# One buffer for all V tiles, the last ones handed over in halves, and an earlier K load, in a decode attention kernel that streams K and V

## Chip, cores, metric

The kernel runs on one core of a Trainium2 chip. The metric is the device time of one execution in microseconds (us). The intervals quoted are 95% intervals.

## The reference

Attention for one new token: 32 query heads, 8 K/V heads, 65,536 keys, head size 128, bf16. Per K/V head `g` there are 4 query heads.

```python
B, Hq, Hkv, Sq, Sk, D = 1, 32, 8, 1, 65536, 128
scores = jnp.einsum("bhqd,bhkd->bhqk", q, k) * D ** -0.5     # k, v repeated 4 times over heads
p = softmax(scores, axis=-1)
out = jnp.einsum("bhqk,bhkd->bhqd", p, v)
```

K and V are 268.4 MB together and every byte is used once. So the question is always the same: is the queue of loads ever empty, and what happens after the last byte has landed?

## The kernel before

Each head has two K tiles and two V tiles of 8.39 MB, written here K(g,b) and V(g,b) or short K10. The buffer `io` has three places of one tile: place 0 for V, places 1 and 2 for K(g,0) and K(g,1). VectorE transposes a K tile in place in four pieces of 4.4 us. TensorE scores it (64 matmuls in a loop of 8 trips, with register addresses), then multiplies the V tile of the head before (64 matmuls in a static block, `wide`). Between heads come the maximum, the exponential on ScalarE and the transposed weights.

A load can be issued only when its place has been used. `s_sc` counts scored eighths of K, `s_vc` counts used V tiles. The loads, all issued in order by SyncE:

```python
    def load_k(g, b):
        SP.wait((s_sc, 16 * g - 8 + 8 * b if g else 0))
        load(k, g, b, 1 + b, (s_ka, s_kb)[b])

    def load_v(g, b):
        if g < G - 1:
            SP.wait((s_vc, 2 * g + b))
            load(v, g, b, 0, s_v[0])
            ...
        elif b == 0:                       # V(7,0): into the place of K(7,0)
            SP.wait((s_sc, 16 * g + 8))
            for i in range(2):
                load(v, g, b, 1, s_u[i], 128 * i, 128 * i + 128)
        else:                              # V(7,1): into the V place, in six cuts
            SP.wait((s_vc, 2 * g))
            ...
    load_k(0, 0); load_k(0, 1); load_v(0, 0)       # on one line each in the kernel
    load_k(1, 0); load_k(1, 1); load_v(0, 1)
    for g in range(2, G):
        for b in range(2):
            load_k(g, b)
            load_v(g - 1, b)
    load_v(G - 1, 0)
    load_v(G - 1, 1)
```

The TensorE loop, cut to its frame. `head_slot` is the argument that sets the slot of the loop's first instruction; with `head_slot={PE: 0}` the loop is called aligned below:

```python
    with nc.Fori(0, G + 1, 1, engines=OrderedEngineSet([PE]), head_slot={PE: 0}) as h:
        ...                                      # wait; add up the last head; zero PSUM by 5 matmuls
        with pe.Fori(0, 2) as j:
            with pe.If(h < G):
                with pe.Fori(0, 8) as n: ...     # scores: 8 matmuls a trip
            with pe.If(h * 2 + j > 1):
                take(s_et, 2)
                with pe.If(h * 2 + j == 2 * G):  # V(7,0), which lies in a K place
                    with pe.Fori(0, SL // UN) as n:
                        ...                      # register addresses
                        for c in range(4):
                            i = pe.matmul(out=vacc[0:16, :, :], ...)
                with pe.Else():
                    ...                          # 64 x wide(ch, tt)
```

## Time and profile before

| | before |
|---|---|
| time, median of 3 first runs (range) | 655.73 us (655.61 to 658.28) |
| span of the profiled run | 655.3 us |
| load queue's share of 16 DMA engines | 94.9% |
| TensorE, VectorE busy | 57%, 52% |
| holes in the loads | 100 to 112 us, and from 636 us to the end |

In the profiles PE is TensorE, DVE is VectorE, ACT is ScalarE; PEq and SPq are the sequencers of TensorE and SyncE, which issue instructions and loads. L339 is line 339 of the kernel.

The page of the profile, in lines: the span; the DMA engines' busy share in 40 slices of 16.4 us, in tenths, and the rate; two queues (packets, MB, share); then two groups of instructions (line, engine, operation, output and inputs, count, busy us, mean ns of one, idle time before them).

```profile
span 655.3 us, 7257 instructions
...
DMA  9999991999999999999999999999999999999970
GB/s 382 448 448 400 436 444 68 448 448 413 420 448 444 440 396 448 444 444 392 448 448 444 424 412 448 444 444 392 445 448 444 416 420 448 448 436 396 443 330 0
...
q1 hardware_dynamic: 5480, 268.44, 94.9%
...
q8 instruction: 1, 0.02, 0.0%
...
L339 PE MATMUL vacc<-io,et 128*16 128x512 bf16 x956 | 55.7, 387 | 5.3 <-PEq L325 5.3
...
L390 PE MATMUL vacc<-io,et 128*16 x64 | 16.7, 384 | 9.6 <-PEq L325 9.6
```

The loads are what fills the time. Two slices stand out: the seventh (68 GB/s) and the last (0). In between 27 tiles pass from 113 to 636 us, that is 433 GB/s, with no moment of 0.3 us or more in which no load is in flight. An estimate from that rate: at 433 GB/s, 268.4 MB take 620 us.

The table of windows shows both holes (columns: window; its length; busy time and count of TensorE, its weight loads, VectorE, ScalarE, GpSimd; granted TensorE clock, as a share of full speed; DMA share; GB/s):

```profile
100.00:112.00 12.00, 9.38 (x88) 3.92 (x88) 0.68 (x2) 0.00 (x0) 0.00 (x0) 1.00 0.00 0
112.00:116.00 4.00, 0.00 (x0) 0.00 (x0) 4.00 (x3) 0.00 (x0) 0.00 (x0) 1.00 1.31 524
...
632.00:636.00 4.00, 2.35 (x10) 0.85 (x10) 0.00 (x0) 0.00 (x0) 0.00 (x0) 1.00 0.97 387
636.00:655.00 19.00, 11.01 (x98) 4.42 (x96) 3.23 (x9) 0.00 (x0) 0.00 (x0) 0.91 0.01 5
```

A window counts each packet of a load whole, where it starts. In the stream a 64 KB packet takes 2.42 us (median) and most of the 16 DMA engines start theirs together, so windows of 2 to 4 us can show shares over 1 (524 GB/s) or low rates with no change in the flow. A hole is certain only where nothing is in flight.

And the timeline tells what ends each (start, duration, engine, line, instruction; in brackets the idle time before it):

```profile
82.32 17.42 DVE L227 STREAM_TRANSPOSE io<-io 128x4096 uint32<-128x4096 uint32 x4 [6.72 <-DMA io<-in_k_dram]
...
107.64 3.63 PE L339 MATMUL vacc<-io,et 128*16 128x512 bf16 x64 [0.27 <-PEq L325]
111.32 0.33 SPq L128 DMA_DIRECT2D io<-in_v_dram  x1
...
642.57 1.02 PE L390 MATMUL vacc<-io,et 128*16 x4 [0.70 <-PEq L325]
645.50 4.92 PE L339 MATMUL vacc<-io,et 128*16 128x512 bf16 x60 [1.91 <-PEq L325]
...
652.88 0.35 SPq L290 DMA_DIRECT2D out_dram<-o  x1
```

V(0,1) can be issued only at 111.32, when V(0,0) has been used; that waits for K(1,0), which was transposed from 82.32 on, when it landed. At the end, the register-addressed loop for V(7,0) needs 1.7 us for every four matmuls (27.3 us for 64, where the static block of V(6,1) took 3.63 us) and is still at work at 642.57. All but a trickle of the loads had landed by 636.2.

### The profile page before, as it was taken

How to read it: one execution, taken by the hardware profiler on the slowest of the kernel's cores; microseconds unless marked ns; L12 is line 12 of the kernel's file. 1: busy time of each engine (PE TensorE's matmuls, PEld its weight loads, DVE VectorE, ACT ScalarE, POOL GpSimd, SP SyncE). 2: the span in 40 equal slices, each digit the busy share in tenths (PEclk: the TensorE clock that was granted, in tenths of full speed). 3: DMA queues.
4: the chain of work that ended last, by engine and by line, in shares of the span. 5: the costliest groups of instructions: out<-in, count | busy, mean ns of one | idle time of the engine just before them, and what ended most of it. 6: DMA issues, size and time to landing. Idle time of an engine off the chain costs nothing. (4 is left out here: it accounts for less than half of the span.)

```text
span 655.3 us, 7257 instructions
## 1 busy us (share of the span) xinstructions
PE 376.2 (57%) x2167; PEld 147.6 (23%) x2167; DVE 342.4 (52%) x226; ACT 23.6 (4%) x65; POOL 7.9 (1%) x40
## 2 busy tenths in 40 slices
PE   1187466764818656284744838266580866628655
PEld 0032122221303222031311313122130322203212
DVE  1588192936439292564808466193733829156201
ACT  0000100010000100001000010001000010000100
POOL 1000000000000000000000000000000000000000
PEclk9999769795978879597895959879596886959898
DMA  9999991999999999999999999999999999999970
GB/s 382 448 448 400 436 444 68 448 448 413 420 448 444 440 396 448 444 444 392 448 448 444 424 412 448 444 444 392 445 448 444 416 420 448 448 436 396 443 330 0
DMA packets 5589, 268.50 MB, mean 410 GB/s; under 512 B 720, under 2 KB 720, under 8 KB 1104
## 3 DMA queue, kind: packets, MB, share of 16 engines
q1 hardware_dynamic: 5480, 268.44, 94.9%
q10 hardware_dynamic: 104, 0.02, 0.0%
q14 instruction: 4, 0.03, 0.0%
q8 instruction: 1, 0.02, 0.0%
HBM read 268.44 MB, written 0.01 MB: 410 GB/s over the span
## 5 line engine op out<-in xcount | busy, mean ns | idle before, releaser
L370 PE MATMUL sc<-io,wz 128*128 x1024 | 272.5, 418 | 217.0 <-PEq L325 174.6
L227 DVE STREAM_TRANSPOSE io<-io 128x4096 uint32<-128x4096 uint32 x64 | 279.5, 4415 | 109.4 <-DMA io<-in_k_dram 109.4
L370 PEld LDWEIGHTS sc<-io,wz 128*128 x1024 | 106.0, 104 | 386.8 <-issue 308.6
L263 DVE STREAM_TRANSPOSE et<-ex 128x512 bf16<-128x512 bf16 x32 | 21.5, 701 | 117.3 <-PE vacc L339 81.3
L339 PE MATMUL vacc<-io,et 128*16 128x512 bf16 x956 | 55.7, 387 | 5.3 <-PEq L325 5.3
L232 DVE TENSOR_REDUCE mx<-sc 128x1 f32<-128x512 f32 x32 | 20.8, 668 | 49.7 <-PE sc L370 49.7
L252 ACT ACTIVATE ex<-sc,nmb 128x512 bf16<-128x512 f32 x32 | 21.6, 685 | 589.8 <-DVE nmb L249 589.8
L339 PEld LDWEIGHTS vacc<-io,et 128*16 128x16 bf16 x956 | 24.6, 91 | 36.3 <-issue 14.1
L390 PE MATMUL vacc<-io,et 128*16 x64 | 16.7, 384 | 9.6 <-PEq L325 9.6
L356 PE MATMUL sc<-zero 128*128 128x512 bf16 x36 | 17.0, 628 | 0.0
L272 DVE TENSOR_SCALAR vs<-vacc,sely 128x128 f32<-128x128 f32 x8 | 2.8, 350 | 24.6 <-PE vacc L339 24.6
L352 PE MATMUL pb<-ls,sel 128*4 128x4 f32 x18 | 1.8, 169 | 19.1 <-PEq L325 19.1
L212 POOL COPY wz<-qT 32x16 bf16<-32x16 bf16 x32 | 6.1, 191 | 520.0 <-PE sc L370 516.7
L414 PE MATMUL pb<-one,nrow 1*128 1x1 f32 x16 | 2.8, 241 | 14.3 <-PEq L325 14.3
L390 PEld LDWEIGHTS vacc<-io,et 128*16 x64 | 5.5, 86 | 21.2 <-issue 17.9
L335 PE MATMUL pf<-vs,sel 128*4 128x128 f32 x20 | 4.2, 295 | 9.9 <-PEq L325 9.2
L275 DVE SCALAR_TENSOR_TENSOR vs<-vacc,sely,vs 128x128 f32<-128x128 f32 x24 | 8.4, 351 | 0.9
L252 ACT ACTIVATION_READ_ACCUMULATOR ex<-sc,nmb 128x1 f32 x32 | 6.5, 202 | 0.0
L352 PEld LDWEIGHTS pb<-ls,sel 128*4 128x4 f32 x18 | 1.2, 86 | 21.6 <-issue 21.4
L414 PEld LDWEIGHTS pb<-one,nrow 1*128 1x128 f32 x16 | 2.3, 182 | 15.6 <-issue 15.6
L356 PE MATMUL vacc<-zero 128*128 128x512 bf16 x9 | 5.7, 634 | 0.0
L356 PEld LDWEIGHTS sc<-zero 128*128 128x128 bf16 x36 | 3.9, 131 | 5.3 <-issue 5.0
(29 smaller groups left out, 23.9 us busy)
## 6 DMA issues: line engine op xcount, KB each, us to landing
io<-in_v_dram SPq DMA_DIRECT2D x3, 4096.0 KB, 38.0
io<-in_v_dram SPq DMA_DIRECT2D x1, 2048.0 KB, 23.6
io<-in_v_dram SPq DMA_DIRECT2D x1, 1024.0 KB, 25.7
io<-in_v_dram SPq DMA_DIRECT2D x1, 512.0 KB, 26.4
io<-in_v_dram SPq DMA_DIRECT2D x2, 256.0 KB, 26.7
io<-in_k_dram SPq DMA_DIRECT2D x16, 47.7
io<-in_v_dram SPq DMA_DIRECT2D x14, 28.9
out_dram<-o ACTq DMA_DIRECT2D x7, 1.0 KB
```

The lines of the kernel that those rows point to most:

```text
L212: gp.tensor_copy(out=wz[r, :, c0:c0 + H].rearrange("p (s w) h -> p s w h", s=2), in_=qTb[r, :, :, g, :],).then_inc(s_w, 1)
L227: dve.transpose(out=part.bitcast(u32), in_=part.bitcast(u32)).then_inc(s_kt, 2)
L232: return DV.mark(dve.tensor_reduce(out=mx[:, b:b + 1], in_=sc[:, 512 * b:512 * b + 512], axis=AX.X, op=ALU.max))
L252: a = act.activation(out=ex[:, b, :], in_=sc[:, 512 * b:512 * b + 512], func=ACT.Exp, bias=nmb[:, :], scale=SCALE, accum_out=ls[:, b:b + 1],)
L263: dve.transpose(out=et[:, i, :], in_=ex[:, 2 * b + i, :]).then_inc(s_et, 1)
L275: i = dve.scalar_tensor_tensor(out=vs[:, :], in0=vacc[:, y, :], scalar=sely[:, y:y + 1], in1=vs[:, :], op0=ALU.mult, op1=ALU.add,)
L335: return pe.matmul(out=fin, lhsT=sel[:, :], rhs=vs[:, :], skip_group_check=True, **kw)
L339: return pe.matmul(out=vacc[32 * c:32 * c + 16, :, :], lhsT=et[:, ch // 2, w0:w0 + 16], rhs=io[:, PS * ch + 4 * tt:PS * ch + 4 * tt + 4, : ...
L356: pe.matmul(out=bank, lhsT=zero[:, 0:P], rhs=zero[:, :], start=True, stop=False, skip_group_check=True,)
L370: i = pe.matmul(out=bass.AP(sc, r_o, [[2048, P], [1, 512]]), lhsT=bass.AP(wz, r_w + ((2 * s + e) * WB - 4 * u), [[4 * WB, P], [1, P]]), rh ...
L390: i = pe.matmul(out=vacc[0:16, :, :], lhsT=bass.AP(et, r_e + c * 32, [[1024, P], [1, 16]]), rhs=bass.AP(io, r_v + c * (4 * D), [[IO, P], [ ...
L414: pe.matmul(out=pb[:, 0:1], lhsT=nrow[:, :, :].rearrange("o x h -> o (x h)"), rhs=one[:, :], start=True, stop=True,).then_inc(s_pe, 1)
```

## The change

Its intent: no hole near 100 us, and no slow loop at the end. V(7,0) and V(7,1) go through the V place like all others. So that the V place does not become a bottleneck at the end, the last V tiles are handed over in halves (`s_vc` now counts half tiles), and K(7,1) comes in quarters. K(0,0) comes in halves and K(1,0) is loaded ahead of V(0,0). Zeroing PSUM moves from TensorE to ScalarE and VectorE, and the softmax of a head is put ahead of collecting the output of the head before. The loop is not aligned any more. The core of the diff:

```diff
+    k_cuts = {(0, 0): [0, 128, 256], (G - 1, 1): [0, 64, 128, 192, 256]}
...
     def load_v(g, b):
-        if g < G - 1:
-            SP.wait((s_vc, 2 * g + b))
+        done = 2 * (2 * g + b)
+        if (g, b) == (G - 1, 1):
+            SP.wait((s_vc, done - 1))
+            load(v, g, b, 0, s_v[0], CUTS[0], CUTS[1])
+            SP.wait((s_vc, done))
+            for lo, hi, s in list(zip(CUTS, CUTS[1:], s_v))[1:]:
+                load(v, g, b, 0, s, lo, hi)
+        elif (g, b) in ((G - 2, 1), (G - 1, 0)):
+            for i in range(2):
+                SP.wait((s_vc, done - 1 + i))
+                load(v, g, b, 0, s_v[i], 128 * i, 128 * i + 128)
...
     load_k(0, 0)
     load_k(0, 1)
-    load_v(0, 0)
-    load_k(1, 0)
-    load_k(1, 1)
-    load_v(0, 1)
-    for g in range(2, G):
+    for g in range(1, G):
         for b in range(2):
             load_k(g, b)
             load_v(g - 1, b)
...
+        if g < G - 1:
+            ACTQ.after(n)
+            ACTQ.mark(act.activation(
+                out=sc[:, :], in_=zero[:, 0:1].to_broadcast([P, 4 * 512]), func=ACT.Copy
+            ))
...
         top()
+        softmax(g)
         if g:
             d_rl = reciprocal(g - 1)
-            DV.wait((s_vc, 2 * g))
+            DV.wait((s_vc, 4 * g))
             collect()
-        softmax(g)
...
-    with nc.Fori(0, G + 1, 1, engines=OrderedEngineSet([PE]), head_slot={PE: 0}) as h:
+    with nc.Fori(0, G + 1, 1, engines=OrderedEngineSet([PE])) as h:
...
-        for bank in [sc[:, 512 * b:512 * b + 512] for b in range(4)] + [
-            vacc[:, :, :].rearrange("p y d -> p (y d)")
-        ]:
-            pe.matmul(
-                out=bank, lhsT=zero[:, 0:P], rhs=zero[:, :], start=True, stop=False,
-                skip_group_check=True,
-            )
...
-                with pe.If(h * 2 + j == 2 * G):
-                    with pe.Fori(0, SL // UN) as n:
...
+                for ch in range(4):
+                    if ch != 1:
+                        take(s_v[max(ch - 1, 0)], 16)
+                    for tt in range(16 if ch < 3 else 12):
...
+                    if ch == 1:
+                        i.then_inc(s_vc, 1)
```

More of the change, by code (lines that the diff above doesn't have):

```diff
@@ L22 @@
 TAIL = 16
-UN = 16
 CUTS = [0, 128, 192, 224, 240, 248, 256]
@@ L76 @@
     wz = sb("wz", [P, 4, WB], bf16)
-    zero = sb("zero", [P, 512], bf16)
+    zero = sb("zero", [P, 1], fp32)
     ident = sb("ident", [P, P], fp32)
@@ L103 @@
     pl, fin = pb[0:H, 8:12], pf[0:H, 0:D]
-    s_q, s_ka, s_kb, s_st = sem("s_q"), sem("s_ka"), sem("s_kb"), sem("s_st")
+    s_q, s_st = sem("s_q"), sem("s_st")
     s_v = [sem(f"s_v{i}") for i in range(len(CUTS) - 1)]
-    s_u = [sem(f"s_u{i}") for i in range(2)]
-    s_un = sem("s_un")
     s_dv, s_ac, s_gp = sem("s_dv"), sem("s_ac"), sem("s_gp")
@@ L113 @@
     )
-    s_sc, s_pe, s_vb, s_vc, s_vu = sem("s_sc"), sem("s_pe"), sem("s_vb"), sem("s_vc"), sem("s_vu")
+    s_sc, s_pe, s_vb, s_vc = sem("s_sc"), sem("s_pe"), sem("s_vb"), sem("s_vc")
     sp, act, dve, gp, pe = nc.sync, nc.scalar, nc.vector, nc.gpsimd, nc.tensor
@@ L130, in load @@
         ).then_inc(s, 16)
+    k_cuts = {(0, 0): [0, 128, 256], (G - 1, 1): [0, 64, 128, 192, 256]}
+    s_k = {(b, lo): sem(f"s_k{b}_{lo}") for b, lo in ((0, 0), (0, 128), (1, 0), (1, 64), (1, 128), (1, 192))}
+    k_count = {}
+    k_ready = {}
     def load_k(g, b):
         SP.wait((s_sc, 16 * g - 8 + 8 * b if g else 0))
-        load(k, g, b, 1 + b, (s_ka, s_kb)[b])
-    def load_v(g, b):
-        if g < G - 1:
-            SP.wait((s_vc, 2 * g + b))
+        cuts = k_cuts.get((g, b), [0, SL])
+        for lo, hi in zip(cuts, cuts[1:]):
+            k_ready[g, b, lo] = key = s_k[b, lo], k_count.get((b, lo), 0) + 16
+            k_count[b, lo] = key[1]
+            load(k, g, b, 1 + b, key[0], lo, hi)
+    def load_v(g, b):
+        done = 2 * (2 * g + b)
[9 more added lines that the diff above has]
+                load(v, g, b, 0, s_v[i], 128 * i, 128 * i + 128)
+            for s in s_v[2:4]:
+                sp.sem_inc(s, 16)
+        else:
+            SP.wait((s_vc, done))
             load(v, g, b, 0, s_v[0])
@@ L141, in load_v @@
                 sp.sem_inc(s, 16)
-        elif b == 0:
-            SP.wait((s_sc, 16 * g + 8))
-            for i in range(2):
-                load(v, g, b, 1, s_u[i], 128 * i, 128 * i + 128)
-        else:
-            SP.wait((s_vc, 2 * g))
-            for lo, hi, s in zip(CUTS, CUTS[1:], s_v):
-                load(v, g, b, 0, s, lo, hi)
     load_k(0, 0)
     load_k(0, 1)
-    load_v(0, 0)
-    load_k(1, 0)
-    load_k(1, 1)
-    load_v(0, 1)
-    for g in range(2, G):
+    for g in range(1, G):
         for b in range(2):
@@ L168 @@
     GP.mark(gp.memset(wz[:, :, :], 0.0))
-    GP.mark(gp.memset(zero[:, :], 0.0))
     n = GP.mark(gp.memset(ident[:, :], 0.0))
@@ L176 @@
     DV.mark(dve.memset(one[:, :], 1.0))
-    dve.memset(ls[:, :], 0.0).then_inc(s_ls, 1)
-    dve.memset(vs[:, :], 0.0).then_inc(s_vs, 2)
+    n = DV.mark(dve.memset(ls[:, :], 0.0))
+    d_zero = DV.mark(dve.memset(zero[:, :], 0.0))
+    DV.mark(dve.memset(vs[:, :], 0.0))
+    for b in range(4):
+        DV.mark(dve.memset(sc[:, 512 * b:512 * b + 512], 0.0))
+    n = DV.mark(dve.memset(vacc[:, :, :], 0.0))
+    DV.after(n)
+    dve.sem_inc(s_ls, 1)
+    dve.sem_inc(s_vs, 2)
     DV.wait((s_gp, p_ident))
@@ L217 @@
     gp.sem_inc(s_w, 4)
-    for i in range(2):
-        GP.wait((s_u[i], 16))
-        gp.sem_inc(s_un, 128 // UN)
     def transposes(g, b):
-        DV.wait(((s_ka, s_kb)[b], 16 * (g + 1)))
         for t0 in range(0, SL, PS):
+            if (g, b, t0) in k_ready:
+                DV.wait(k_ready[g, b, t0])
             part = io[:, (1 + b) * SL + t0:(1 + b) * SL + t0 + PS, :].rearrange("p t d -> p (t d)")
@@ L256, in softmax @@
             ACTQ.mark(a)
+        n = ACTQ.n
+        if g == 0:
+            ACTQ.wait((s_dv, d_zero))
+        if g < G - 1:
[3 more added lines that the diff above has]
+            ))
         act.wait_ge(s_ac, ACTQ.n)
@@ L261, in weights @@
         for i in range(2):
-            DV.wait((s_ac, 4 * g + 2 * b + i + 1))
+            DV.wait((s_ac, 5 * g + 2 * b + i + 1))
             dve.transpose(out=et[:, i, :], in_=ex[:, 2 * b + i, :]).then_inc(s_et, 1)
@@ L269, in reciprocal, with collect @@
         return DV.mark(dve.reciprocal(out=rl[:, :], in_=l4[:, :]))
-    def collect():
+    def collect(last=False):
         n = DV.mark(dve.tensor_scalar_mul(out=vs[:, :], in0=vacc[:, 0, :], scalar1=sely[:, 0:1]))
@@ L278, in collect @@
             )
-            if y < 3:
-                n = DV.mark(i)
-            else:
-                i.then_inc(s_vs, 1)
+            n = DV.mark(i)
+        if not last:
+            DV.after(n)
+            n = DV.mark(dve.memset(vacc[:, :, :], 0.0))
+        DV.after(n)
+        dve.sem_inc(s_vs, 1)
     def finish(g, n_pe, d_rl):
@@ L295 @@
         if g:
-            DV.wait((s_vc, 2 * g - 1))
+            DV.wait((s_vc, 4 * g - 2))
             weights(g - 1, 1)
@@ L312 @@
             finish(g - 1, 4 * g + 5, d_rl)
-    DV.wait((s_vu, SL // UN))
+    DV.wait((s_vc, 4 * G - 2))
     weights(G - 1, 1)
     d_rl = reciprocal(G - 1)
-    DV.wait((s_vb, 2 * G - 1))
-    collect()
+    DV.wait((s_vb, 2 * G))
+    collect(last=True)
     finish(G - 1, 4 * G + 3, d_rl)
@@ L383 @@
                 take(s_et, 2)
-                with pe.If(h * 2 + j == 2 * G):
-                    with pe.Fori(0, SL // UN) as n:
-                        r_v = n * (UN * D) + SL * D
-                        r_e = (n // 8) * 512 + (n // 4) % 2 * 16 + (n % 4) * 128
-                        take(s_un, 1)
-                        for c in range(4):
-                            i = pe.matmul(
-                                out=vacc[0:16, :, :],
-                                lhsT=bass.AP(et, r_e + c * 32, [[1024, P], [1, 16]]),
-                                rhs=bass.AP(io, r_v + c * (4 * D), [[IO, P], [1, 4 * D]]),
-                                start=False, stop=False, skip_group_check=True,
-                            )
-                        i.then_inc(s_vu, 1)
-                with pe.Else():
-                    for ch in range(4):
-                        if ch != 1:
-                            take(s_v[max(ch - 1, 0)], 16)
-                        for tt in range(16 if ch < 3 else 12):
-                            if (ch, tt) == (3, 8):
-                                take(s_v[3], 16)
-                            i = wide(ch, tt)
-                    i.then_inc(s_vb, 1)
-                    with pe.If(h < G):
-                        for tt in range(12, 16):
-                            i = wide(3, tt)
-                        i.then_inc(s_vc, 1)
+                for ch in range(4):
+                    if ch != 1:
+                        take(s_v[max(ch - 1, 0)], 16)
+                    for tt in range(16 if ch < 3 else 12):
+                        if (ch, tt) == (3, 8):
+                            take(s_v[3], 16)
+                        i = wide(ch, tt)
+                    if ch == 1:
+                        i.then_inc(s_vc, 1)
+                i.then_inc(s_vb, 1)
+                with pe.If(h * 2 + j < 2 * G + 1):
+                    for tt in range(12, 16):
+                        i = wide(3, tt)
+                    i.then_inc(s_vc, 1)
         with pe.If(h < G):
```

## The prediction

> What bounds the kernel now. The page gives the queue of the loads (q1) 94.9% of the span, the TensorE 57%, the VectorE 52%: it streams K and V. 16 K and 16 V tiles of 8.39 MB go through three buffers. In the table of 4 us windows the DMA is busy from about 2 us to 636 us except for one hole, about 99.5 to 113 us (0 GB/s from 100 to 112). From 113 to 636.2 us 27 tiles pass, 19.4 us each (433 GB/s). So the time is: 32 tiles x 19.4 us, the hole (13 us), and a tail of 19 us from the last landing (636) to 655.3.
>
> The hole. The second V tile may load only when the first has been used. In the timeline V(0,0) is used at 107.6 to 111.3, because K(1,0) landed only at 82.3, behind V(0,0), which was loaded before anybody could use it. From the start of K(1,0)'s VectorE transposes to the V hand-over is 29.0 us (82.3 to 111.3).
>
> The tail. V(7,0) goes to a K buffer and is multiplied by the register-addressed loop: 64 matmuls take 27.3 us (617.3 to 644.6; 1.7 us per 4 matmuls of 0.26 us), where the static block takes 3.63 us for 64. V(7,1), landed at 636, waits for that; then weights transposes, 60 matmuls, collection and store run to 655.3.
>
> The change.
> 1. Load order K00 K01 K10 V00 K11. K00 lands at 24, K01 at 43.6, K10 at 63, V00 at 82, K11 at 101. K00 in halves is scored by about 39 instead of 49.6, so K10 is issued in time. K01 is scored at 43.6 + 25.1 (as K(1,1): 112.55 to 137.6) = 68.7; softmax and first weights 4.8 us more (70.8 to 75.6) = 73.5; then the 29.0 us chain: V00 used at 102.5, not 111.3. Hole: 3 to 4 us left. Gain 8.8 us, all critical.
> 2. V(7,0) and V(7,1) through the one V buffer in halves and the static block; K(7,1) in quarters. By the same durations K(7,1) is scored 16.7 us after its landing, V(6,1) is half used 1 us before its own end of loading and V(7,0)'s first half is issued then: about 1 us of DMA gap. After the last landing there remain a few matmuls, collection (1.5 us), gather, scaling, store: 5 to 6 us instead of 19. Gain 13.5 less 1.
> 3. Zeroing of PSUM moves from 5 matmuls (1.89 + 0.63 us per head) to one ScalarE copy (estimate 2 us, from 0.69 us per 512 columns) and a VectorE memset: TensorE idles there waiting for K anyway. Worth 0.
> 4. Softmax ahead of collect: not critical. Worth 0.
> 5. No alignment.[...] Before, the page shows one 16 KB packet on q8 and nothing during the loop; no stall is visible. The new loop is shorter (I count about 200 slots). [...]TensorE then waits for K, with 7 to 9 us of slack between V hand-over and the end of queued loads (141.5 against about 151).[...]
>
> Sum: 655.7 - 8.8 - 12.5 = 634.4.
>
> Checks: hole under 5 us near 102; q1 share near 98%; no L390-like loop; last landing 626 to 630; end 5 to 6 us later[...].
>
> Wrong if: [...]smaller loads run slower.

## The result, and the profile after

| | before | after |
|---|---|---|
| time, median (range, runs) | 655.67 us (655.31 to 658.28, 4) | 635.92 us (635.68 to 636.36, 4) |
| ratio | | 0.9691 (0.9666 to 0.9717) |
| span of the profiled run | 655.3 us | 634.2 us |
| share of the load queue | 94.9% | 98.4% |
| loads wholly idle near 100 us | 10.8 us | 1.2 us |
| last load to the result's write | 15.5 us | 3.8 us |

A ratio is the mean time of one kernel's fast runs over that of the other's fast runs of the same rounds, so it is not quite the ratio of the medians. The last two rows are read from the start and end of the load queue's single transfers in the trace; the two differences (9.6 and 11.7 us) add up to 21.3 us, and the spans differ by 21.1 us. The 1.2 us is that of one profile; `after_again`, the same kernel, shows 2.0.

The page after:

```profile
span 634.2 us, 7031 instructions
...
DMA  8999999999999999999999999999999999999896
GB/s 364 455 438 434 426 397 397 446 413 459 401 459 401 463 401 459 438 422 455 405 459 401 459 403 459 434 422 459 405 455 409 455 409 451 406 438 417 372 429 262
...
q1 hardware_dynamic: 6200, 268.44, 98.4%
...
q8 instruction: 1, 0.02, 0.0%
...
L359 PE MATMUL vacc<-io,et 128*16 128x512 bf16 x1020 | 65.3, 409 | 20.1 <-PEq L345 20.1
```

No slice is empty now, the register-addressed group is gone, and the static block has its 64 matmuls (1020 instead of 956 records). The windows at the same two places, and one new one:

```profile
98.00:100.00 2.00, 2.00 (x44) 0.97 (x36) 0.00 (x0) 0.00 (x0) 0.00 (x0) 1.00 0.30 131
100.00:102.00 2.00, 0.64 (x12) 0.11 (x4) 1.31 (x3) 0.00 (x0) 0.00 (x0) 1.00 1.38 459
102.00:104.00 2.00, 0.00 (x0) 0.00 (x0) 2.00 (x1) 0.00 (x0) 0.00 (x0) 1.00 0.19 66
586.00:588.00 2.00, 1.60 (x32) 0.54 (x23) 0.59 (x2) 0.00 (x0) 0.00 (x0) 1.00 0.19 82
588.00:590.00 2.00, 0.91 (x20) 0.50 (x24) 0.00 (x0) 0.00 (x0) 0.00 (x0) 1.00 0.86 262
...
624.00:628.00 4.00, 2.95 (x28) 0.66 (x28) 0.00 (x0) 0.00 (x0) 0.00 (x0) 0.50 0.99 396
628.00:634.00 6.00, 2.86 (x22) 1.86 (x22) 1.74 (x5) 0.00 (x0) 0.00 (x0) 0.72 0.07 25
```

Only a remnant of the hole at 100 us is left; the bulk of the loading stops about 6 us before the end, not 19. The thin stretch at 586 to 590 us is new: it is the hand-over from V(6,1) to V(7,0). The timeline after:

```profile
71.96 17.38 DVE L237 STREAM_TRANSPOSE io<-io 128x4096 uint32<-128x4096 uint32 x4
...
97.01 3.63 PE L359 MATMUL vacc<-io,et 128*16 128x512 bf16 x64
100.68 0.33 SPq L125 DMA_DIRECT2D io<-in_v_dram  x1
...
585.70 1.90 PE L359 MATMUL vacc<-io,et 128*16 128x512 bf16 x32
589.09 1.91 PE L359 MATMUL vacc<-io,et 128*16 128x512 bf16 x32 [1.49 <-PEq L345]
...
631.79 0.35 SPq L310 DMA_DIRECT2D out_dram<-o  x1
```

K(1,0) is transposed from 71.96 instead of 82.32. Now it waits not for its landing (61.5) but for VectorE, which is busy with the softmax and the first weights of head 0 until then (from 67.25, when the last scores are there, to 72.03). So V(0,1) is issued at 100.68 instead of 111.32. V(6,1) is used in two halves (585.70 and 589.09), with the first half handed back between them.

### The profile page after: what moved, and what is told of

Read it like the earlier page. It is cut to its first block, busy times and chain, and to the rows that moved or that the text cites. A ratio compares the mean times of both kernels' runs of the same rounds, so it can differ in the third digit from the quotient of the medians.

```text
span 634.2 us, 7031 instructions
## 1 busy us (share of the span) xinstructions
PE 349.6 (55%) x2122; PEld 139.5 (22%) x2122; DVE 347.5 (55%) x239; ACT 36.7 (6%) x72; POOL 7.3 (1%) x39
## 3 DMA queue, kind: packets, MB, share of 16 engines
q1 hardware_dynamic: 6200, 268.44, 98.4%
## 5 line engine op out<-in xcount | busy, mean ns | idle before, releaser
L359 PE MATMUL vacc<-io,et 128*16 128x512 bf16 x1020 | 65.3, 409 | 20.1 <-PEq L345 20.1
L359 PEld LDWEIGHTS vacc<-io,et 128*16 128x16 bf16 x1020 | 26.6, 93 | 57.8 <-issue 36.7
L251 DVE TENSOR_REDUCE m<-pt 1x4 f32<-1x128 f32 x8 | 2.2, 279 | 22.5 <-PE pt L413 22.5
L272 ACT ACTIVATE sc<-zero 128x2048 f32<-128x2048 f32 x7 | 13.2, 1880 | 0.3
L355 PEld LDWEIGHTS pf<-vs,sel 128*4 128x4 f32 x20 | 1.3, 87 | 27.2 <-issue 27.2
L300 DVE MEMSET vacc<- 128x512 f32 x7 | 3.4, 485 | 1.3 <-DVE vs L293 1.3
L259 DVE COPY nmb<-pb 128x1 f32<-128x1 f32 x8 | 1.3, 157 | 4.3 <-PE pb L415 4.3
(27 smaller groups left out, 21.3 us busy)
```

What stands on the lines that cost most here:

```text
L272: ACTQ.mark(act.activation(out=sc[:, :], in_=zero[:, 0:1].to_broadcast([P, 4 * 512]), func=ACT.Copy))
L300: n = DV.mark(dve.memset(vacc[:, :, :], 0.0))
L355: return pe.matmul(out=fin, lhsT=sel[:, :], rhs=vs[:, :], skip_group_check=True, **kw)
L359: return pe.matmul(out=vacc[32 * c:32 * c + 16, :, :], lhsT=et[:, ch // 2, w0:w0 + 16], rhs=io[:, PS * ch + 4 * tt:PS * ch + 4 * tt + 4, : ...
```

## The experiments

Twelve runs, all correct. Names beginning with `a_` are edits of the kernel after, with `b_` of the kernel before. One caution for reading them: the runs of the kernel before fall in two groups, about 655.0 to 656.5 and 657.5 to 658.9 us, and how many fall in each differs. So experiments on the kernel after are compared with `after_again` (`a_nohalf_v` and `a_k71_whole` ran on another chip than it); those on the kernel before by the ratio and the spans.

The kept profiles show two differences that go with the groups. In `before` and `b_order_half` the last block of 60 matmuls took 4.92 and 4.95 us, with a granted clock of 0.50 for 3.4 us of it; in `b_noalign` and `b_order` it took 3.42 and 3.41 us at 1.00. And in the first two the time is 3.4 and 3.3 us longer than the span, with a second packet on the instruction queue q8 after the last instruction; in the other two it is 2.1 us longer, without that packet. Why an execution takes the one or the other is open. A comparison of spans is therefore fair only between profiles with the same end.

### The control: after_again

No edit; the kernel after once more, on the same chip as `a_slot0_same_chip`, `a_k_halves` and `a_zero_pe`.

> The kernel after once more, unchanged, beside the next three on one chip, because the three runs with an alignment all came out at 637.4 us on another chip, against 635.9 for after on its own. If that 1.4 us belongs to the chip: 637 us here or equal to the aligned kernel of this call. If it belongs to the alignment: 635.5 to 636.4.

Measured: 636.09 us (636.05 to 636.70, 5 runs), span 634.5. So the 1.4 us that the aligned kernels had shown did not belong to the chip; see below.

### The head: b_order and b_order_half

`b_order` is the kernel before with the new load order alone:

```diff
-    load_v(0, 0)
-    load_k(1, 0)
-    load_k(1, 1)
-    load_v(0, 1)
-    for g in range(2, G):
+    for g in range(1, G):
```

> The kernel before with the new load order alone (K00 K01 K10 V00 K11 V01), K00 still one transfer. My account: K00 is scored at 49.6 us, so K10 cannot be issued before and the queue is dry from about 43 to 51 us; V00 is then used at about 104.6, before the queue runs dry at 109, so the old hole is gone. Net 5 to 6 us faster than before: 649 to 651 us, hole of about 8 us near 45 and none near 105. Rival (order alone closes the hole, the split does nothing): 645 to 647 us.

Measured: 652.34 us, before 657.53 on that chip, ratio 0.9927 (0.9903 to 0.9951), so 4.8 us faster than this mix of runs of before, which were mostly of the upper group. The profile of `b_order` has the short end, so the fair partners are the two runs of the lower group (655.87 and 655.91): 3.5 us faster. The wholly idle time at the head says the same, 7.2 us instead of 10.8. So the expected 5 to 6 us, and the expected time, were missed; the mechanism is as stated. The hole has moved, from 100 to 42 us, because K(1,0) may load only when K(0,0) has been scored:

```profile
42.00:50.00 8.00, 5.93 (x25) 2.30 (x24) 6.08 (x2) 0.00 (x0) 0.00 (x0) 1.00 0.00 0
50.00:52.00 2.00, 0.65 (x3) 0.38 (x4) 2.00 (x1) 0.00 (x0) 0.00 (x0) 1.00 1.56 524
100.00:104.00 4.00, 3.74 (x60) 1.64 (x62) 0.00 (x0) 0.00 (x0) 0.00 (x0) 1.00 0.95 410
```

`b_order_half` adds the split of K(0,0) into two halves with a semaphore each:

```diff
+    k_cuts = {(0, 0): [0, 128, 256]}
...
-        load(k, g, b, 1 + b, (s_ka, s_kb)[b])
+        cuts = k_cuts.get((g, b), [0, SL])
+        for lo, hi in zip(cuts, cuts[1:]):
+            ...
+            load(k, g, b, 1 + b, key[0], lo, hi)
```

> The kernel before with the new load order and K(0,0) in two halves. My account, corrected by the trace of after (hole fully idle for 1.2 us instead of 10.8): 9.6 us faster than before, 645.5 to 647 us, tail unchanged at about 19 us. Rival (the gain at the head is given back later, because steady state waits anyway): under 4 us faster.

Measured: 649.22 us, ratio 0.9874 (0.9849 to 0.9899), so 8.3 us faster than before; span 646.7 against 655.3, two profiles with the same long end: 8.6 us. The gain is about 1 us short of the expected 9.6, and the absolute time missed its expectation: that was reckoned down from the lower group, and the profiled run of this kernel has the long end. Loads are wholly idle for 1.9 us near 102 us instead of 10.8:

```profile
100.00:102.00 2.00, 2.00 (x44) 0.99 (x40) 0.00 (x0) 0.00 (x0) 0.00 (x0) 1.00 0.00 0
```

The rival (given back later) falls. Order and split are both needed: wholly idle 10.8 us before, 7.2 with the order alone, 1.9 with both.

### The end: a_nohalf_v and a_k71_whole

`a_nohalf_v` is the kernel after with whole-tile waits for the last three V tiles:

```diff
-            SP.wait((s_vc, done - 1))
-            load(v, g, b, 0, s_v[0], CUTS[0], CUTS[1])
             SP.wait((s_vc, done))
+            load(v, g, b, 0, s_v[0], CUTS[0], CUTS[1])
...
-        elif (g, b) in ((G - 2, 1), (G - 1, 0)):
+        elif False:
```

> The kernel after, but V(6,1), V(7,0) and the start of V(7,1) again wait for the whole tile before them. From the trace of after: V(7,0) is issued at 591 instead of 587.6 (2.3 us after the queue ran dry, plus the start), V(7,1) only when V(7,0) is used, 5 to 6 us after the queue ran dry. Expected 8 to 9 us slower than after: 643 to 645 us. Rival (half hand-over is decoration, the static block alone closes the tail): 636 to 637 us.

Measured: 650.92 us (650.56 to 651.27), 14.8 us slower than `after_again`. The direction is right; the size, expected at 8 to 9 us, was not. The transfers show two holes of 6.9 and 7.0 us. The first two lines here are of the timeline:

```profile
588.93 5.32 PE L358 MATMUL vacc<-io,et 128*16 128x512 bf16 x64 [3.33 <-PEq L344]
...
616.24 5.57 PE L358 MATMUL vacc<-io,et 128*16 128x512 bf16 x64 [17.34 <-PEq L344]
```

and these of the windows:

```profile
590.00:592.00 2.00, 2.00 (x24) 0.83 (x20) 0.00 (x0) 0.00 (x0) 0.00 (x0) 0.50 0.00 0
...
616.00:618.00 2.00, 1.76 (x20) 0.70 (x24) 0.00 (x0) 0.00 (x0) 0.00 (x0) 0.50 0.00 0
```

The expectation took the time of V(7,0)'s issue from the kernel after (591), where the first half of V(6,1) is already used when the second lands. Without halves all 64 matmuls come after the landing, and they are slow: 5.3 to 5.6 us instead of 3.63, as the granted clock is 0.50 for much of each block: 0.87, 0.50 and 0.77 in the windows from 588 to 594 us, 0.50, 0.50 and 0.95 from 616 to 622. TensorE had stood idle for 3.33 and 17.34 us just before; what lowers the clock was not tested. Half-tile hand-over is worth more here (14.8 us) than the whole early hole (10.8 us). The rival (decoration) falls.

`a_k71_whole` loads K(7,1) as one transfer:

```diff
-    k_cuts = {(0, 0): [0, 128, 256], (G - 1, 1): [0, 64, 128, 192, 256]}
+    k_cuts = {(0, 0): [0, 128, 256]}
```

> The kernel after with K(7,1) as one transfer. It lands at about 569 us instead of beginning to be transposed at 560.7, so its scoring ends 8 to 9 us later (594 instead of 585.7), V(6,1) is handed on late and the queue is dry from about 588.7 to 598: 7 to 9 us slower, 643 to 645 us. Rival (K in quarters does not matter, because V(6,1) lands only at 588.7): within 1 us of after.

Measured: 645.17 us (644.78 to 645.61), 9.1 us slower than `after_again`, and the transfers are wholly idle for 9.1 us. Expected was 7 to 9. The timeline:

```profile
569.42 8.77 DVE L237 STREAM_TRANSPOSE io<-io 128x4096 uint32<-128x4096 uint32 x2 [8.66 <-DMA io<-in_k_dram]
...
594.48 3.63 PE L359 MATMUL vacc<-io,et 128*16 128x512 bf16 x64
596.42 2.05 SPq L125 DMA_DIRECT2D io<-in_v_dram  x2
```

and one window in the hole:

```profile
590.00:592.00 2.00, 1.92 (x8) 0.77 (x8) 0.00 (x0) 0.00 (x0) 0.00 (x0) 1.00 0.00 0
```

With whole tiles, V(6,1) has long landed (the windows from 588 to 596 us show 0 GB/s) when TensorE comes to it at 594.48 (585.70 with quarters). The V place is held not by its load but by the scores ahead of it. So the split of a K tile is what frees a V place.

### Zeroing: a_zero_pe

The kernel after, with PSUM zeroed by five matmuls per head as before, and without the ScalarE copy and the VectorE memsets:

```diff
-            ACTQ.mark(act.activation(
-                out=sc[:, :], in_=zero[:, 0:1].to_broadcast([P, 4 * 512]), func=ACT.Copy
-            ))
...
+        for bank in [sc[:, 512 * b:512 * b + 512] for b in range(4)] + [
+            vacc[:, :, :].rearrange("p y d -> p (y d)")
+        ]:
+            pe.matmul(out=bank, lhsT=zero[:, 0:P], rhs=zero[:, :], start=True, stop=False, ...)
```

> The kernel after with the zeroing of PSUM given back to TensorE (5 matmuls against zeros per head) in place of the ScalarE copy and VectorE memsets. My account says that this part of the change is worth nothing: within 0.5 us of after_again. Rival (zeroing matmuls were on the path between softmax and the next scores): 2 us or more slower.

Measured: 636.61 us (636.12 to 637.63, 4 runs), 0.5 us above `after_again`, ranges overlapping. No sign of the 2 us of the rival. This part is worth nothing measurable by itself, as far as this run can tell: its profiled execution also has the q8 packet of the next section at another time (36 to 44 us, about 371 us in `after`), so the two are not quite separated.

### Alignment: a_slot0, a_slot0_same_chip, a_slot100, a_slot222, b_noalign

The first four are the kernel after with the loop head on a chosen slot; the last is the kernel before without its alignment:

```diff
-    with nc.Fori(0, G + 1, 1, engines=OrderedEngineSet([PE])) as h:
+    with nc.Fori(0, G + 1, 1, engines=OrderedEngineSet([PE]), head_slot={PE: 0}) as h:    # or 100, 222
```

> The kernel after, with the alignment given back[...]. Theory 1[...]: same time, 635 to 637 us, ratio to after within 0.3%. Rival[...]: 2 us or more faster, 634 or less, and the last V matmuls or the hand-over at 100.7 us come earlier.

> The kernel after, with the loop head put on slot 100 on purpose[...]. Theory 1[...]: within 0.5% of after, 635 to 639 us. Rival[...]: 645 us or more, and a TensorE wait of 3 us or more ahead of the first scoring matmul at j = 1[...].

> The kernel after, with the loop head put on slot 222[...]. Theory A[...] the time goes above 700 us. Theory B[...]: no change, 635 to 639 us. My guess is B at 60%, because the trace of after shows only one q8 packet though its loop is not aligned.

> The kernel before, with only the alignment taken away[...]. If alignment never matters here: 655 to 657 us, within 0.3% of before. If crossing costs[...]: 658 to 670 us, because the chain to the hand-over at 111 us and the tail from 617 us are on the critical path[...].

> The kernel after with the loop head at slot 0, again, on the same chip as after_again. If alignment costs 1.4 us: 1 to 2 us above after_again. If the chip made the difference: within 0.5 us of after_again. I expect the second.

Measured: `a_slot0` 637.40, `a_slot100` 637.33, `a_slot222` 637.51 us on one chip; `a_slot0_same_chip` 637.82 (636.83 to 637.98, 5 runs) beside `after_again` 636.09 (636.05 to 636.70). `b_noalign` 655.73 us (4 runs, 655.38 to 655.98), no difference from the lower group of before.

Two things follow. First, which of the three slots the loop head is on made no difference: 637.40, 637.33 and 637.51 us. The profiles of `a_slot0_same_chip`, `a_slot100` and `a_slot222` have one packet on the instruction queue q8 (between 0 and 8, 36 and 44, 22 and 30 us) and none from there to 635 us. The times above 700 us that the expectation of slot 222 held possible did not come.

Second, and against my expectation, alignment costs 1.7 us here (636.09 against 637.82, with ranges that do not touch). The place to look is that one packet. The DMA view of the first 8 us of `a_slot0_same_chip` has it:

```profile
q8 instruction: 1, 0.02, 0.7%
```

For `a_slot100` it is found between 36 and 44 us:

```profile
q8 instruction: 1, 0.02, 0.8%
```

The landing of K is seen in the first transposes. For `after_again`, which has no such packet from 0 to 8 or from 36 to 44 us:

```profile
13.22 8.77 DVE L237 STREAM_TRANSPOSE io<-io 128x4096 uint32<-128x4096 uint32 x2 [7.13 <-DMA io<-in_k_dram]
...
42.29 4.45 DVE L237 STREAM_TRANSPOSE io<-io 128x4096 uint32<-128x4096 uint32 x1 [10.58 <-DMA io<-in_k_dram]
```

for `a_slot0_same_chip`:

```profile
14.46 8.77 DVE L237 STREAM_TRANSPOSE io<-io 128x4096 uint32<-128x4096 uint32 x2 [8.37 <-DMA io<-in_k_dram]
...
43.84 4.45 DVE L237 STREAM_TRANSPOSE io<-io 128x4096 uint32<-128x4096 uint32 x1 [10.90 <-DMA io<-in_k_dram]
```

and for `a_slot100`:

```profile
13.14 8.77 DVE L237 STREAM_TRANSPOSE io<-io 128x4096 uint32<-128x4096 uint32 x2 [7.05 <-DMA io<-in_k_dram]
...
43.77 4.45 DVE L237 STREAM_TRANSPOSE io<-io 128x4096 uint32<-128x4096 uint32 x1 [12.19 <-DMA io<-in_k_dram]
```

With the packet in the first 8 us, the first half of K(0,0) lands 1.2 us later. With the packet at 36 to 44 us, K(0,0) lands as early as without (13.14 against 13.22), and K(0,1) is 1.5 us late (43.77 against 42.29). Slot 222 has its packet between 22 and 30 us and K(0,1) at 43.40; `a_zero_pe`, not aligned but with a longer loop, has it at 36 to 44 us and K(0,1) at 43.78. In all of them V(0,1) is issued at 101.9 to 102.3 instead of 100.7 to 100.8. So the delay comes where the packet comes, and in these profiles a q8 packet in the head goes with a shift of the critical chain, seen at the issue of V(0,1), by 1.0 to 1.6 us.

Two things limit this account. The packet at 371 us in `after` goes with a smaller delay, 0.65 us: read from the single transfers, the 8.39 MB then under way land 20.0 us after the 8.39 MB before, where 19.35 us is usual. And `a_zero_pe` took 637.63 us in the profiled execution, which has the packet in the head, but 636.12 to 636.87 in the other three. Only one execution of a kernel is profiled, so where the packet fell in those is not known. That the packet is the whole cost of alignment is likely, not shown.

What else stays open: why the kernel after has its one q8 packet only at about 371 us (at 371.1, 16 KB), and what it carries. The trace does not name the engine of that queue; that it serves TensorE is the conclusion, from its time changing with the placement of TensorE's loop (between 0 and 8, 22 and 30, 36 and 44 us for slots 0, 222, 100). Why alignment makes no difference in the kernel before fits the same account (without alignment its packet only moves, to 46 to 56 us, still in the head), but that was not tested further.

### The holes that were left: a_k_halves

The kernel after with two more K tiles in halves:

```diff
-    k_cuts = {(0, 0): [0, 128, 256], (G - 1, 1): [0, 64, 128, 192, 256]}
+    k_cuts = {(0, 0): [0, 128, 256], (0, 1): [0, 128, 256], (G - 1, 0): [0, 128, 256], (G - 1, 1): [0, 64, 128, 192, 256]}
```

> The kernel after with two more K tiles loaded in halves: K(0,1) and K(7,0). Theory (what is left beside streaming is the hole at 101 us and the thin stretch at 586 to 590 us, both because scoring hands V on too late): V(0,0) is used by about 92 us, before the queue runs dry at 101, V(6,1) is half used by about 583, before its own landing, so both holes go: 4 to 5 us less, 631 to 632 us, ratio to after about 0.993. Rival (the holes are bandwidth dips or the cost of starting a transfer): no change, within 1 us.

Measured: 632.30 us (632.21 to 632.54, 5 runs), against `after_again` 636.09 (636.05 to 636.70): 3.8 us or 0.6% faster, and 0.9626 of before (0.9605 to 0.9648). It is the best version. The timeline:

```profile
89.29 3.63 PE L359 MATMUL vacc<-io,et 128*16 128x512 bf16 x64
92.96 0.33 SPq L125 DMA_DIRECT2D io<-in_v_dram  x1
...
578.35 1.90 PE L359 MATMUL vacc<-io,et 128*16 128x512 bf16 x32
```

V(0,1) is issued at 92.96, while K(1,1) is still loading, and V(6,1) is half used at 580.25 (578.35 + 1.90), before its second half has landed. No moment of 0.3 us or more without a load is left before the last one lands. The rival (start-up costs or dips of bandwidth) falls.

## Why the prediction was right

The prediction said 634.4 us; 635.92 was measured.

- **What bounds the kernel** (load queue, two holes): right. Removing the two holes is the gain: 9.6 and 11.7 us of idle queue went, and the span fell by 21.1 us. That the two fit so closely is partly chance, as two smaller terms cancel. Counted over all 16 DMA engines, with the moments in which only some were idle, the early hole fell from 13.0 to 1.5 us (11.5 us), and the thin stretch at 586 to 590 us, which is new, takes 1.9 us: 11.5 - 1.9 + 11.7 = 21.3 us as well.
- **Step 1, the head.** Predicted: V(0,0) used at 102.5, hole of 3 to 4 us left, gain 8.8. Seen: V(0,1) issued at 100.68, loads wholly idle for 1.2 us, gain 9.6 in the trace; `b_order_half` alone gained 8.3. The chain was right. It came out 1.8 us early mainly because the landing of K(0,1) was taken from the trace of before (43.6), where the q8 packet falls in the first 8 us (at 5.3); after, it was 42.1.
- **Step 2, the end.** Predicted 13.5 less 1. Seen: the time between the last load and the result's write fell by 11.7 us, from 15.5 to 3.8, and there is a thin stretch of 4 us at 586 to 590. The prediction counted the old tail from 636, where the bulk had landed; the last packet came at 638.1. The thin stretch cost about 2 us, not 1: 1.9 by the idle time of the 16 engines, 2.4 by the rough rates of the windows, (4 x 433 - 2 x 82 - 2 x 262) / 433. From the last landing (628.7) to the end it is 5.5 us, within the predicted 5 to 6. `a_nohalf_v` (14.8 us) and `a_k71_whole` (9.1 us) show that the static block is only a part of this step: without either split most of the gain would have been lost to new holes. What the static block gives with V(7,0) left in the K place was not run.
- **Steps 3 and 4.** Zeroing was predicted to be worth 0, and `a_zero_pe` measures 0.5 us with overlapping ranges (and the doubt said there). The order of softmax and collection was not tested alone; no new wait of loads can be put down to it.
- **Step 5, alignment.** The value (nothing) was nearly right; the reasons were not shown by any run. Slots 0, 100 and 222 took the same time (637.3 to 637.5 us). Alignment costs the new kernel 1.4 to 1.7 us, likely through one q8 packet that falls into the head (not shown), so leaving it out gave the new kernel a little. The prediction had expected no gain there. A check on more packets on q8 did not come true: one packet within the span before, one after.
- **The sum.** The terms were read from a profiled run with a span of 655.3 us, which belongs to the slower group (it took 658.7 us), but were taken off the median of 655.7. Span against span the estimate, 655.3 - 21.3 = 634.0, is within 0.2 us of the 634.2 seen; median against median the gain is 19.8. Part of the good fit is therefore luck: the head gained more than predicted, the hand-over at the end cost more, and the base was mixed.

## What to carry to other kernels

In a kernel that streams, list the times at which the load queue is empty and name for each the instruction whose end allows the next load; that chain, not any engine's busy share (TensorE 57% before, 55% after), is what this change shortened. Splitting a load pays where the work on its first part lets an earlier buffer go free: here the cuts of K freed the place of V (9.1 us lost without those of K(7,1), 3.8 us gained by two more). When costing a change from one profiled run, take the base from that same run, and check whether it is a typical one.
